# Two transformer layers on one core: whole-tile transposes of the attention output, paired half-zero V copies, first loads from two queues, single-tile GLU at first

## The chip, the core and the metric

The kernel runs on one core of a Trainium2 chip. A core has a matrix engine (PE; its weight loads are shown as PEld), a vector engine (DVE), a scalar engine (ACT), GpSimd (POOL) and a queue engine (SP), which here issues DMAs. Each engine takes its instructions strictly in order; semaphores make one wait for another. The metric is the device time of one execution in microseconds, as the median of several runs.

## What is computed

Two identical layers on a sequence of 2048 rows with 512 features in bf16. Each is attention with 32 heads of 16 features, where a query sees itself and the 255 keys before it, and then a gated MLP of width 1792, each on a layer norm of its input and each added to it:

```python
h = x + A(layernorm(x));  x = h + B(layernorm(h))      # twice, same weights
# A: q, k, v of x @ wqkv; 32 heads of 16
scores = einsum("bhqd,bhkd->bhqk", q, k) * 16 ** -0.5
mask = (i - j >= 0) & (i - j < 256)
o = softmax(where(mask, scores, -1e9)) @ v;  A = o @ wo
# B
B = (sigmoid(x @ w_gate) * (x @ w_up)) @ w_down
```

## The kernel before, in words

The rows are cut into 16 tiles of 128 per layer. All weights and the activations stay in SBUF. Every instruction is laid out by a planner that runs when the program is built (`Plan`, from L169): it keeps a clock of its own, an assumed duration for each instruction and each DMA (`act_ns`, `dve_ns`, `DMA_LATENCY`, `FETCH`, `EXTRA`), and at each step gives an engine the task of the lowest priority number whose inputs are ready on that clock. What it writes down is then the fixed order of each engine. Where the chip is slower than assumed, the engine waits at that place, and all behind it in its order waits too. For a DMA of `ns` and `nbytes` the planner reckons from issue to landing `ns` + EXTRA + bytes/250 + DMA_LATENCY nanoseconds (L230 to L262).

- **Start** (`loads`, L371): tiles 0 to 3 of x come one by one (two DMAs each, even and odd halves of the rows), then wq in three parts, then the rest of x, all issued by SP. GLU weights follow from 18 us of the plan's clock on, one DMA each 1.2 us. Tiles 0 to 3 are normalised (`layer_norm`, L474) and turned on PE (L517); all later ones are turned by a DMA transpose into `xnT` (L529).
- **Projections**: q and k per group of four tiles (L555, L577), v per tile (L609). V is copied into `Vaug`, 18 columns per head: 16 of V and ones, so that the value product also sums the softmax's denominator.
- **Attention**, tile by tile: a *visit* is one round of score products into `Sps` (kinds A at L821, R at L831, S at L841) and one exponential on ACT over 128x2048 scores (L872). A tile has five visits, the last of a layer two. `pick` (L951) does not start a visit before 2.9 or 3.2 us (PACE) have gone by on the plan's clock; other PE work is put between. The kind R gives the edges of the window, which are multiplied with copies of V of which half is zero (`Vlo`, `Vhi`; `half_values`, L1039): per tile two DMAs for each, issued by SP.
- **After the value products** (`values`, L874, half a tile's heads at a time; `after_values`, L905): a copy out of PSUM to `OTs` (L539/L541), a DMA transpose to `Oq` (L916), reciprocal and product on DVE (L922, L923), a DMA transpose to `OnT` (L927). When both halves have come, the output projection (L693) adds to x, and the tile is normalised for the GLU.
- **GLU** (`gate_up_unit`, L627, `down_unit`, L660): units of two tiles, 256 columns wide: eight products into one PSUM bank (L633), tanh on ACT (L644), the product on DVE (L647), and per tile 14 products with w_down (L666). GLU is the filler: it has the lowest rank for PE (`rank`, L1116). So it starts when two tiles have been through attention.
- Where PE has nothing to do within the first 85 us of the plan's clock, four 128-wide products of the identity are put in (`keep_warm`, L1024).

Of the kernel before, what the change touches and what calls it, by code (L numbers as in the profile page):

```python
# [25 lines left out]
VS = 18  # L26
VW = H * VS + 32
UNITS = 8
EDGES = 4
# [71 lines left out]
EXTRA = {"ACT": 40, "DVE": 10, "POOL": 30, "SP": 50}  # L101
# [3 lines left out]
DMA_LATENCY = 1200  # L105
FETCH = (1200, 1300)
# [39 lines left out]
class Task:  # L146


    __slots__ = ("engines", "fn", "prio", "done", "can", "began", "seq", "ends", "port")

    def __init__(self, engines, fn, prio, can, port):
        self.engines, self.fn, self.prio, self.can, self.port = engines, fn, prio, can, port
        self.done, self.began, self.ends = Event(), False, None
# [15 lines left out]
class Plan:  # L169
# [60 lines left out]
    def begin(self, t, e):  # L230
# [9 lines left out]
        if e == "SP":  # L240
# [12 lines left out]
    def count(self, n):  # L253

        if (self.issued + 2 * n) // 256 > self.issued // 256:
            self.fetched = self.now
        self.issued += 2 * n

    def dma(self, ns, nbytes, fn, deps=(), prio=5, after=0):
# [4 lines left out]
        return self.task({"SP": ns}, go, deps, prio, None, after)  # L264
# [30 lines left out]
class Net:  # L295


    def __init__(self, ctx, tc, A_x, wqkv, wo, w_gate, w_up, w_down, out):
# [27 lines left out]
        self.edge = [big.tile([P, 2, H // 2, HP], BF16, name=f"edge{i}") for i in range(EDGES)]  # L326
        self.Vlo = [big.tile([P, VW], BF16, name=f"Vlo{i}") for i in range(2)]
        self.Vhi = [big.tile([P, VW], BF16, name=f"Vhi{i}") for i in range(2)]
# [17 lines left out]
        ring("OTs", 2, [P, 4, P])  # L346
        ring("Oq", 2, [P, 4, P])
        ring("Rt", 2, [P, 4, 4, 1], F32)
        ring("On", 2, [P, 4, 4, 16])
        ring("OnT", 3, [P, 2, P])  # L350
# [20 lines left out]
    def loads(self, A_x, wqkv, wo, w_gate, w_up, w_down):  # L371
# [16 lines left out]
        def load(dst, src, nbytes, after=0, deps=(), prio=2):  # L388
            ns = max(450, 40 + nbytes / 1024 * 0.95)
            return pl.dma(ns, nbytes, lambda: nc.sync.dma_start(out=dst, in_=src), deps, prio, after).done  # L390

        for t in range(NBG):
            self.has_x[t] = load_x(self.xsb[:, t:t + 1, :], slice(t, t + 1), 1, 0)
        for i, k in enumerate("qkv"):
            h = slice(i * D, (i + 1) * D)
            self.has_wq[k] = load(self.wq[:, :, h], wq_src[:, :, h], D * D * 2, prio=0 if k != "v" else 1)
# [5 lines left out]
        gap = 1200  # L402
# [31 lines left out]
    def later_constants(self):  # L434
# [27 lines left out]
        def zeros(e):  # L462
            for i in range(2):
                nc.gpsimd.memset(self.Vlo[i][:], 0.0)
                nc.gpsimd.memset(self.Vhi[i][:], 0.0)
# [3 lines left out]
        self.has_zeros = pl.task({"POOL": 2800}, zeros, prio=7).done  # L469
# [80 lines left out]
    def q_unit(self, L, g, cq):  # L550
# [8 lines left out]
        def evac(u):  # L559
# [3 lines left out]
                self.banks[u.bank][:].rearrange("p (t k z) -> p t z k", z=2, k=HP)), [u.done], 3)  # L563
# [8 lines left out]
    def k_unit(self, L, g, cq):  # L572
# [8 lines left out]
        def evac(u):  # L581
# [12 lines left out]
            a = pl.task({"ACT": act_ns(TGW), "DVE": dve_ns(TGW)}, cp, [u.done], 3, lambda: self.has("kt"))  # L594
            b = pl.task({"DVE": 620}, split, [a.done], 3, port=True)
# [8 lines left out]
    def v_unit(self, L, t):  # L604
# [8 lines left out]
        def evac(u):  # L613
# [3 lines left out]
                e, dst, self.banks[u.bank][:].rearrange("p (i e c) -> p e i c", e=2, c=16)), [u.done, self.has_ones[gi % 3]], 3)  # L617
# [9 lines left out]
    def gate_up_unit(self, L, t0, fc, chunk):  # L627
        nc, pl, key = self.nc, self.pl, ("g", L, t0 // NBG)
        c0 = (t0 % NBG) * P

        def steps(bank):
            pt = self.banks[bank][:].rearrange("p (i w) -> p i w", i=2)
            return [(mm_ns(GW), lambda i=i, w=w, kt=kt: nc.tensor.matmul(  # L633
                pt[:, i, :], lhsT=w[:, kt, fc * P:(fc + 1) * P], rhs=self.xnT[key][0][:, kt, c0:c0 + GW],
                start=kt == 0, stop=kt == KT - 1)) for i, w in enumerate((self.wg, self.wu)) for kt in range(KT)]

        def evac(u):
# [12 lines left out]
            a = pl.task({"ACT": act_ns(GW)}, tanh, [u.done], 2, lambda: self.has("th"))  # L650
            b = pl.task({"DVE": dve_ns(GW)}, mult, [a.done], 1)
            b.done.then(lambda: (self.give(box["th"]), self.h_ready[L, t0, fc].fire()))
            return b.done

        a, b = self.has_gu[fc // 2]
        needs = [self.xn_ready[key, t] for t in range(t0, t0 + GT)] + [a, b, self.h_free[chunk]]
        self.h_free[chunk] = self.h_used[L, t0, fc]
        return Unit(("g", L, t0, fc), steps, needs, True, evac)

    def down_unit(self, L, t, chunks):  # L660
        nc, pl = self.nc, self.pl
        t0 = t - t % GT
        o = (t % GT) * P

        def mm(bank, fc):
            nc.tensor.matmul(self.banks[bank][:], lhsT=self.hT[:, chunks[fc], o:o + P], rhs=self.wd[:, fc, :],  # L666
                             start=fc == 0, stop=fc == FC - 1)
            if t == t0 + GT - 1:
# [20 lines left out]
    def oproj_unit(self, L, t, st):  # L689
        nc, pl = self.nc, self.pl  # L690

        def steps(bank):
            return [(mm_ns(D), lambda c=c: nc.tensor.matmul(  # L693
                self.banks[bank][:], lhsT=st[c // 2][0][:, c % 2, :], rhs=self.wot[:, c, :],
                start=c == 0, stop=c == KT - 1)) for c in range(KT)]

        def evac(u):
            u.done.then(lambda: [self.give(b) for b in st.values()])
# [37 lines left out]
    def visit_exp(self, s):  # L736
# [9 lines left out]
        elif j >= EDGES:  # L746
            i = j - EDGES + 2 if (j - EDGES) % NT < NT - 2 else j - EDGES
            deps += [self.pv_done[divmod(i, NT) + (h,)] for h in range(2)]
# [503 lines left out]
```

## Time and profile before

| | |
|---|---|
| runs | 590.3 us median of 3 (589.15 to 590.78) |
| profiled execution | 593.61 us, of which its trace spans 591.9 us |
| PE busy | 547.8 us, 93% of the span |
| PE weight loads, DVE, ACT, POOL | 364.9, 407.6, 410.2, 64.1 us |
| mean granted PE clock | 0.983 |
| DMA | 38.24 MB in 111752 packets |

A row of a group of instructions gives the line of the code, the engine, the tiles written and read, the count, the busy time in all and the mean length of one, and then the idle time of the engine just before them with what ended it. In the timeline a row begins with its start and its length in us, and an idle stretch stands in brackets. In a table by stages each engine has its busy microseconds within the stage, then come the granted clock, the share of the time in which the DMA engines were busy, and GB/s. Products on PE overlap, so their lengths don't add up; the distance of their starts is read from rows of many in a run.

### The profile page before, as it was taken

To read this page: it belongs to the slowest core of one execution; us is meant where nothing else is said; L and a number is where in the kernel's file an instruction comes from. 1 tells how busy PE (TensorE), PEld (TensorE's weight loads), DVE (VectorE), ACT (ScalarE), POOL (GpSimd) and SP (SyncE) were. 2 spreads that over 40 slices of the span, in tenths; PEclk is the share of its full clock that TensorE was granted. 3 is DMA by queue.
4 is the path that set the end of the run, shared out by engine and by line. 5 is a ranking of instruction groups with operands and counts; after the bars stand their busy time and mean duration, and the time that the engine had idled before them with its cause. 6 is when DMAs were issued, how large, how long until landed. Compare 5 with 4: busy or idle time off the path is not lost.

```text
span 591.9 us, 24275 instructions
## 1 busy us (share of the span) xinstructions
PE 547.8 (93%) x10717; PEld 364.9 (62%) x10808; DVE 407.6 (69%) x931; ACT 410.2 (69%) x480; POOL 64.1 (11%) x149
## 2 busy tenths in 40 slices
PE   6979899998889998998899998999989999999997
PEld 5456577665566666565366664756557665667774
DVE  4838657797766877755877586786667876556642
ACT  2667678887858887876687766867687786765221
POOL 5202101131101111100201002100000000000100
PEclk7979999999989999999999998999999999999999
DMA  6869522232321132113431124212341113213100
GB/s 203 227 164 179 65 55 44 58 65 58 70 53 34 35 57 46 38 43 45 73 64 32 32 56 66 48 26 52 65 85 44 43 35 81 51 44 65 37 19 27
DMA packets 111752, 38.24 MB, mean 65 GB/s; under 512 B 88864, under 2 KB 111648, under 8 KB 111648
## 3 DMA queue, kind: packets, MB, share of 16 engines
q1 hardware_dynamic: 111648, 36.70, 30.1%
q8 instruction: 84, 1.38, 1.0%
q14 instruction: 20, 0.16, 0.1%
HBM read 9.70 MB, written 2.10 MB: 20 GB/s over the span
## 4 chain that ended last, share of the span: by engine, by line
PE 70%; DMA 13%; DVE 7%; ACT 4%; issue 3%; SPq 1%; POOL 1%; DVEq 0%; ACTq 0%
PE bank L633 27%; PE bank L666 11%; PE bank L899 7%; DMA Oq<-OTs 5%; PE bank L555 5%; PE bank L577 5%; PE Sps L821 5%; DMA xnT<-xn 5%; PE bank L693 4%; PE bank L609 3%; DMA OnT<-On 2%; PE bank L1028 2%; PE Sps L831 2%; ACT PTring L872 2%; ACT edge L872 1%
## 5 line engine op out<-in xcount | busy, mean ns | idle before, releaser
L872 ACT ACTIVATE PTring<-Sps 128x2048 bf16<-128x2048 f32 (+1 forms) x122 | 225.9, 1851 | 32.0 <-PE Sps L821 31.4
L633 PE MATMUL bank<-xnT,wg 128*128 128x256 bf16 x896 | 138.5, 274 | 2.3 <-DMA xnT<-xn 1.6
L633 PE MATMUL bank<-xnT,wu 128*128 128x256 bf16 x896 | 139.2, 273 | 0.0
L647 DVE SCALAR_TENSOR_TENSOR hT<-th,bank 128x256 bf16<-128x256 bf16 x224 | 86.9, 416 | 39.2 <-ACT th L644 38.9
L666 PE MATMUL bank<-wd,hT 128*128 128x512 bf16 x395 | 108.4, 380 | 4.8 <-DMA OnT<-On 1.6
L644 ACT ACTIVATE th<-bank 128x256 bf16<-128x256 f32 x224 | 79.7, 389 | 44.2 <-PE bank L633 39.5
L633 PEld LDWEIGHTS <-wg 128*128 128x128 bf16 x896 | 84.1, 98 | 30.1 <-issue 4.6
L633 PEld LDWEIGHTS <-wu 128*128 128x128 bf16 x896 | 86.4, 98 | 14.1 <-issue 1.0
L488 POOL TENSOR_SCALAR st<-st 128x1 f32<-128x1 f32 x64 | 19.6, 306 | 485.6 <-DVE st L484 485.6
L872 ACT ACTIVATE edge<-Sps 128x2048 bf16<-128x2048 f32 (+1 forms) x32 | 56.7, 1772 | 20.8 <-PE Sps L831 20.6
L539 ACT CAST OTs<-bank 128x512 bf16<-128x512 f32 x52 | 38.2, 734 | 46.2 <-PE bank L899 45.2
L666 PEld LDWEIGHTS <-hT 128*128 128x128 bf16 x448 | 42.4, 98 | 37.7 <-DVE hT L647 2.8
L762 DVE TENSOR_TENSOR PTring<-PTring,mask 128x1024 bf16<-128x1024 bf16 x64 | 43.9, 686 | 30.2 <-ACT PTring L872 30.0
L899 PEld LDWEIGHTS <-Vaug 128*32 128x32 bf16 x2880 | 44.9, 97 | 22.3 <-issue 21.0
L899 PE MATMUL bank<-PTring,Vaug 128*32 128x64 bf16 (+1 forms) x2880 | 53.5, 204 | 3.4 <-DVE PTring L762 1.6
L821 PE MATMUL Sps<-qT,kTp 32*128 32x64 bf16 (+3 forms) x1856 | 48.2, 219 | 4.6 <-DMA xnT<-xn 1.9
L483 DVE BATCH_NORM_STATS2 st<-xsb 128x6 f32<-128x512 bf16 x64 | 43.9, 686 | 2.7 <-DMA xsb<-in_A_x_dram 2.2
L762 DVE TENSOR_TENSOR edge<-edge,maske 128x1024 bf16<-128x1024 bf16 x60 | 40.8, 685 | 6.9 <-ACT edge L872 6.9
L899 PE MATMUL bank<-edge,Vlo 128*32 128x64 bf16 x1024 | 45.0, 195 | 0.0
L699 DVE TENSOR_TENSOR xsb<-xsb,bank 128x512 bf16<-128x512 bf16 x32 | 21.9, 685 | 33.2 <-PE bank L693 27.0
L821 PEld LDWEIGHTS <-kTp 32*128 32x128 bf16 x1856 | 24.8, 93 | 29.1 <-issue 25.7
L899 PE MATMUL bank<-edge,Vhi 128*32 128x64 bf16 x896 | 41.3, 194 | 0.0
(61 smaller groups left out, 589.9 us busy)
## 6 DMA issues: line engine op xcount, KB each, us to landing
Vlo<-Vaug SPq DMA_DIRECT2D x64, 36.0 KB, 1.8
out_dram<-xsb SPq DMA_DIRECT2D x32, 64.0 KB, 1.9
Vhi<-Vaug SPq DMA_DIRECT2D x56, 36.0 KB, 2.5
wg<-in_B_w_gate_dram SPq DMA_DIRECT2D x7, 256.0 KB, 3.5
wu<-in_B_w_up_dram SPq DMA_DIRECT2D x7, 256.0 KB, 3.8
wd<-in_B_w_down_dram SPq DMA_DIRECT2D x2, 896.0 KB, 7.2
wq<-in_A_wqkv_dram SPq DMA_DIRECT2D x3, 512.0 KB, 6.2
xsb<-in_A_x_dram SPq DMA_DIRECT2D x6, 256.0 KB, 6.5
```

Of the source, the lines that this page charges most:

```text
L483: nc.vector.bn_stats(out=st[:, 0:6], in_=self.xsb[:, t, :])
L539: self.nc.scalar.copy(out=out, in_=in_)
L555: return [(mm_ns(TGW), lambda kt=kt: nc.tensor.matmul(self.banks[bank][:], lhsT=self.wq[:, kt, cq * P:cq * P + P], rhs=self.xnT[key][0][:, ...
L577: return [(mm_ns(TGW), lambda kt=kt: nc.tensor.matmul(self.banks[bank][:], lhsT=self.wq[:, kt, D + cq * P:D + cq * P + P], rhs=self.xnT[ke ...
L633: return [(mm_ns(GW), lambda i=i, w=w, kt=kt: nc.tensor.matmul(pt[:, i, :], lhsT=w[:, kt, fc * P:(fc + 1) * P], rhs=self.xnT[key][0][:, kt ...
L644: nc.scalar.activation(out=box["th"][0][:], in_=pt[:, 0, :], func=AF.Tanh, scale=0.5)
L647: nc.vector.scalar_tensor_tensor(out=self.hT[:, chunk, :], in0=box["th"][0][:], scalar=1.0, in1=pt[:, 1, :], op0=ALU.add, op1=ALU.mult)
L666: nc.tensor.matmul(self.banks[bank][:], lhsT=self.hT[:, chunks[fc], o:o + P], rhs=self.wd[:, fc, :], start=fc == 0, stop=fc == FC - 1)
L762: done = pl.task({"DVE": dve_bf_ns(1024)}, lambda e: nc.vector.tensor_tensor(out=r, in0=r, in1=m.to_broadcast([P, 16, HP]), op=ALU.mult), ...
L821: nc.tensor.matmul(self.sps[:, m, o:o + n * HP], lhsT=kTp[32 * m:32 * m + 32, i, tt, e, :], rhs=self.qT[32 * m:32 * m + 32, i, q0:q0 + n * ...
L872: nc.scalar.activation(out=out, in_=src, func=AF.Exp, scale=scale)
L899: nc.tensor.matmul(o, lhsT=Va[:, c0:c0 + 32], rhs=p(h), start=k == 0 or t == 0, stop=k == len(parts) - 1 or t == 0, tile_position=(0, 32 * g))
```

## The change

**Turning the attention output.** The two halves of a tile are copied into one `OTs` of 8x128; one DMA transpose turns both (256 KB), one reciprocal and one product follow, and one transpose to `OnT`. `OTs`, `Oq` and `On` have one buffer each instead of two of half the size, `OnT` two instead of three.

**Half-zero V copies.** `Vd` holds two tiles; per pair of tiles two DMAs for the low and two for the high copy, when V of both tiles is there. V takes 17 columns per head instead of 18. The edge tiles are six slots of one tile, with the heads in another order.

**First loads.** ACT issues the three parts of wq, in the order k, q, v; SP issues x in pairs of tiles at the same time. GLU weights come one each 1.6 us.

**GLU.** Tiles 0 and 1 of the first layer are units of one tile: two feature chunks of 128 columns for gate and two for up share a bank, so 16 products of 128 columns instead of 8 of 256. Tanh and product on DVE stay 256 wide.

**The planner's numbers.** Longer DMAs (1500 instead of 1200 ns, 70 instead of 50 per issue), a shorter delay after an instruction fetch but SP held for 900 ns by it, other priorities for copies, up to four GLU units in PSUM instead of three, and projections may be drawn ahead by eight visits instead of six.

```diff
-VS = 18
+VS = 17
-EXTRA = {"ACT": 40, "DVE": 10, "POOL": 30, "SP": 50}
+EXTRA = {"ACT": 40, "DVE": 10, "POOL": 30, "SP": 70}
-DMA_LATENCY = 1200
-FETCH = (1200, 1300)
+DMA_LATENCY = 1500
+FETCH = (1200, 800)
...
             self.fetched = self.now
+            if self.free["SP"] > self.now:
+                self.free["SP"] += 900
...
-        ring("OTs", 2, [P, 4, P])
-        ring("Oq", 2, [P, 4, P])
-        ring("OnT", 3, [P, 2, P])
+        ring("OTs", 1, [P, 8, P])
+        ring("Oq", 1, [P, 8, P])
+        ring("OnT", 2, [P, 4, P])
...
-        for t in range(NBG):
-            self.has_x[t] = load_x(self.xsb[:, t:t + 1, :], slice(t, t + 1), 1, 0)
-        for i, k in enumerate("qkv"):
+        for i, k in enumerate("kqv"):
...
+            self.has_wq[k] = load(self.wq[:, :, h], wq_src[:, :, h], D * D * 2, prio=0, queue="ACT")
+        for t in range(0, NBG, 2):
+            self.has_x[t] = self.has_x[t + 1] = load_x(self.xsb[:, t:t + 2, :], slice(t, t + 2), 2, 0)
...
-        gap = 1200
+        gap = 1600
...
-        b = pl.dma(1190, 131072, turn, [a.done], 3)
+        if half == 0:
+            return
+        b = pl.dma(1800, 262144, turn, [box[0], box[1]], 3)
...
-        d = pl.dma(1190, 65536, turn2, [c.done], 3)
+        d = pl.dma(1190, 131072, turn2, [c.done], 3)
...
+                to, of = dst[e * HP:e * HP + HP, :, e * n:e * n + n], V[z:P:2, o:o + 2, e * n:e * n + n]
+                parts.append(pl.dma(580, HP * n * 4, lambda to=to, of=of: nc.sync.dma_start(out=to, in_=of), deps, 3).done)
...
-                if u.ready() and self.can_go(u) and not (u.on_act and busy_act >= 3):
+                if u.ready() and self.can_go(u) and not (u.on_act and busy_act >= 4):
...
-            return lead / 1000 if lead <= 6 else 6 + lead / 1000
+            return lead / 1000 if lead <= 8 else 6 + lead / 1000
...
+                k = 1 if L * NT + t0 < 2 or L * NT + t0 >= 2 * NT - 0 else 2
+                m = FC * k // 2
...
+                gs += [self.gate_up_unit(L, t0, k, (i,) if k == 2 else (2 * i, 2 * i + 1), chunks[i]) for i in range(m)]
```

What this does to the order of the instructions shows at three places. The first is SP from its first DMA on, before the change (`wg`, `wu`, `wd` are the GLU's weights):

```order
L390 DMA xsb<-in_A_x_dram 64x512 x8
L390 DMA wq<-in_A_wqkv_dram 128x4x512 x3
L390 DMA xsb<-in_A_x_dram 64x4x512 x6
L390 DMA wot<-in_A_wo_dram 128x4x512
L529 DMA_TRANSPOSE xnT_104<-xn_101 128x4x128
L390 DMA wg<-in_B_w_gate_dram 128x4x256
...
L390 DMA wg<-in_B_w_gate_dram 128x4x256
L1050 DMA Vlo_86<-Vaug_77 64x288
L390 DMA wu<-in_B_w_up_dram 128x4x256
L529 DMA_TRANSPOSE xnT_104<-xn_101 128x4x128
```

SP after it:

```order
L394 DMA xsb<-in_A_x_dram 64x2x512 x4
L394 DMA xsb<-in_A_x_dram 64x4x512 x6
L394 DMA wot<-in_A_wo_dram 128x4x512
L1062 DMA Vl_83<-Vaug_77 64x2x272 x2
L1062 DMA Vh_85<-Vaug_77 64x2x272 x2
L394 DMA wg<-in_B_w_gate_dram 128x4x256
L394 DMA wu<-in_B_w_up_dram 128x4x256
L536 DMA_TRANSPOSE xnT_101<-xn_98 128x4x128
```

The wq loads have left SP, and the V copies of tiles 0 and 1 stand ahead of every GLU weight; before, the first of them stood behind five. The second place is ACT at its first copies, before:

```order
L539 COPY xnT_103<-bank_64 128x4x128
L539 COPY xnT_103<-bank_65 128x4x128
L539 COPY xnT_103<-bank_66 128x4x128
L539 COPY xnT_103<-bank_67 128x4x128
L539 CAST kt_106<-bank_64 128x512
L539 CAST qT<-bank_65 128x512
```

and after:

```order
L394 DMA wq<-in_A_wqkv_dram 128x4x512 x3
L546 ACT_TABLE_LOAD
L546 COPY xnT_100<-bank_64 128x4x128
L546 COPY xnT_100<-bank_65 128x4x128
L546 CAST Vaug_77<-bank_66 128x32x16
L546 COPY xnT_100<-bank_67 128x4x128
L546 CAST Vaug_77<-bank_64 128x32x16
L546 CAST kt_103<-bank_67 128x512
```

V of tiles 0 and 1 now comes ahead of the first k and q. The third is ACT at its first tanh (`th`), before; the exponential of `edge` in these rows belongs to tile 4, whose number is the fifth edge written:

```order
L539 CAST Vaug_79<-bank_65 128x32x16
L872 ACTIVATE PTring<-Sps 128x16x128 x3
L644 ACTIVATE th_108<-bank_67 128x256
L644 ACTIVATE th_109<-bank_64 128x256
L644 ACTIVATE th_110<-bank_65 128x256
L872 ACTIVATE edge_82<-Sps 128x4x8x64
```

and after, where the `edge` is that of tile 3:

```order
L883 ACTIVATE PTring<-Sps 128x8x2x128 x2
L546 CAST Vaug_79<-bank_64 128x32x16
L883 ACTIVATE PTring<-Sps 128x8x2x128
L653 ACTIVATE th_105<-bank_65 128x256
L883 ACTIVATE edge<-Sps 128x4x2x256
L653 ACTIVATE th_106<-bank_66 128x256
```

Before, 20 exponentials stand ahead of the first tanh, 19 visits ahead of the first gate product; after, 15 and 15.

More of the change, by code (lines that the diff above doesn't have):

```diff
@@ L256, in count, with dma @@
             self.fetched = self.now
+            if self.free["SP"] > self.now:
+                self.free["SP"] += 900
+                self.at(self.free["SP"])
         self.issued += 2 * n
-    def dma(self, ns, nbytes, fn, deps=(), prio=5, after=0):
+    def dma(self, ns, nbytes, fn, deps=(), prio=5, after=0, queue="SP"):
         def go(e):
@@ L262, in go @@
             self.dma_free = max(self.dma_free, self.now + ns) + nbytes / 250.0
-        return self.task({"SP": ns}, go, deps, prio, None, after)
+        t = self.task({queue: ns}, go, deps, prio, None, after)
+        t.transfer = True
+        return t
     def run(self, pe):
@@ L745, in visit_exp @@
             deps += [self.ring_free(L, t, h) for h in range(2)]
[L746 to L749 removed]
+        elif j >= 2:
+            deps += [self.pv_done[divmod(j - 2, NT) + (h,)] for h in range(2)]
+        x = pl.task({"ACT": EXP_NS}, lambda e: self.exp(L, t, kind, i), [d for d in deps if d is not None], 1)
         U = UNIT[j]
@@ L906, in after_values @@
         nc, pl = self.nc, self.pl
-        box = {}
+        box = self.outs.setdefault((L, t), {})
         def move(e):
-            box["OTs"] = self.take("OTs")
-            self.copy(e, box["OTs"][0][:].rearrange("p c (k z) -> p c z k", z=2),
+            if "OTs" not in box:
+                box["OTs"] = self.take("OTs")
+            self.copy(e, box["OTs"][0][:, 4 * half:4 * half + 4, :].rearrange("p c (k z) -> p c z k", z=2),
                       self.banks[bank][:].rearrange("p (c z k) -> p c z k", z=2, k=HP))
```

169 lines of the change are left out of this document (87 added, 82 removed).

## Prediction

> **What bounds the kernel now.** I read the stages first, then PE's waits, then the timeline where the stages differ. The stages (columns: length; busy time of PE, weight loads, DVE, ACT, POOL; clock; DMA share; GB/s):
>
> ```profile
> 0.00:83.00 83.00, 70.00 (x1261) 46.53 (x1271) 54.16 (x126) 51.30 (x47) 17.83 (x49) 0.92 0.69 155
> 83.00:550.00 467.00, 440.36 (x9191) 291.79 (x9266) 336.36 (x767) 348.95 (x407) 44.70 (x96) 0.99 0.26 52
> 550.00:592.00 42.00, 37.45 (x270) 26.58 (x272) 17.10 (x38) 9.96 (x26) 1.58 (x4) 1.00 0.10 27
> ```
>
> From 83 us on PE is busy for 440.36 of 467 us, ACT for 75%: PE is the bound there and in the tail. The first stage looks busy too, but a table of the identity products alone shows what that is:
>
> ```profile
> 16.00:83.00 67.00, 19.49 (x284) 17.18 (x284) 0.00 (x0) 0.00 (x0) 0.95 0.69 142
> 83.00:592.00 509.00, 1.01 (x12) 0.76 (x12) 0.00 (x0) 0.00 (x0) 0.99 0.25 50
> ```
>
> 284 of them fill PE until there is GLU work, and almost none are needed after. The timeline gives the first projection, a run of 40 fillers, the first gate product and a round of scores; the chain gives gate and down products back to back:
>
> ```profile
> 12.19 0.61 PE L577 MATMUL bank<-xnT,wq 128*128 128x512 bf16 x1
> 50.58 2.41 PE L1028 MATMUL bank<-ident 128*128 128x128 bf16 x40
> 82.65 0.49 PE L633 MATMUL bank<-xnT,wg 128*128 128x256 bf16 x3
> 83.07 0.40 PE L821 MATMUL Sps<-qT,kTp 32*128 32x64 bf16 x16
> 572.95 1.75 PE bank L633 x16
> 581.24 3.02 PE bank L666 x14
> ```
>
> So a 128-wide product takes about 58 ns (2.41 less the last one's length of 0.2, over 39, is 57), a 256-wide one 109 ns (1.75/16), and a 512-wide one 216 (3.02/14). The sum of PE's useful work is fixed; the end comes earlier by what PE stops losing, before 82.65 us in waits and fillers, after it in waits. These are its waits that end with a DMA or with what a late DMA held up (who waited for whom; total, times, longest):
>
> ```profile
> PE bank L693 <- DMA OnT<-On: 6.9, 4, 3.4
> PE bank L555 <- DMA xnT<-xn: 3.0, 2, 2.0
> PE bank L1028 <- ACT Vaug L539: 2.1, 1, 2.1
> PE Sps L821 <- DMA xnT<-xn: 1.9, 1, 1.9
> PE bank L666 <- DMA OnT<-On: 1.6, 1, 1.6
> PE bank L633 <- DMA xnT<-xn: 1.6, 4, 0.7
> PE Sps L821 <- ACT PTring L872: 1.4, 1, 1.4
> ```
>
> **Part by part, as time on PE.** *First loads.* SP spends 5.06 us issuing x and only then issues wq:
>
> ```profile
> 0.79 5.06 SPq L390 DMA_DIRECT2D xsb<-in_A_x_dram  x8
> 5.89 1.69 SPq L390 DMA_DIRECT2D wq<-in_A_wqkv_dram  x3
> 8.35 2.51 DVE L505 TENSOR_SCALAR xn<-xsb,st 128x512 bf16<-128x512 bf16 x4
> 9.43 1.56 ACT L539 COPY xnT<-bank 128x512 bf16<-128x512 bf16 x3 [7.36 <-PE bank L517]
> 5.00:6.00 1.00, 1.00 (x21) 0.97 (x18) 0.95 (x6) 0.00 (x0) 0.61 (x1) 1.00 0.27 75
> 9.00:10.00 1.00, 1.00 (x12) 1.00 (x11) 0.86 (x3) 0.57 (x2) 1.00 (x4) 0.50 1.10 390
> ```
>
> The wq issues cost ACT 1.7 us inside its 7.36 us of idleness; without that cover, the 1.7. But DVE, 0.95 busy in 5:6, sets the last xn (10.9 us) as much as the loads do, and five V products now stand between the last turned tile and the first k. I take 1 us of gain. Ends: 3 us gained if PE no longer falls to half clock here (0.50 in 9:10; twelve 512-wide products at 216 instead of twice that are 2.6), 2 lost if ten V products at half clock (4.3 us) are only half covered. DMA engines were 0.27 busy in 5:6, so the queue that issues was the narrow place. The Trainium skill (DMA: Bandwidth & Descriptors, "Issuing engines are not separate DMA queues") says a second issuing engine saves only the sequencer's time, since all transfers share the same DMA engines; by it this part saves at most the 5.06 us of issues that stand before wq's now. The 1.10 share in 9:10 agrees that the transfers then crowd each other, and DVE's part leaves 1 of it.
>
> *V copies ahead of the GLU weights.* Now SP places the first copy of V among the 256 KB loads:
>
> ```profile
> 25.60 0.54 SPq L1050 DMA_DIRECT2D Vlo<-Vaug  x1
> 29.98 1.07 ACT L539 CAST Vaug<-bank 128x512 bf16<-128x512 f32 x2 [4.25 <-DMA Vlo<-Vaug]
> 32.89 0.61 PE L821 MATMUL Sps<-qT,kTp 32*128 32x128 bf16 x24 [1.44 <-ACT PTring L872]
> 33.43 2.74 PE L1028 MATMUL bank<-ident 128*128 128x128 bf16 x24
> 35.97 0.63 PE L555 MATMUL bank<-xnT,wq 128*128 128x512 bf16 x1
> 36.82 1.49 PE L555 MATMUL bank<-xnT,wq 128*128 128x512 bf16 x3 [0.22 <-issue]
> 34.00:36.00 2.00, 2.00 (x22) 2.00 (x20) 0.54 (x1) 1.43 (x1) 0.00 (x0) 0.50 0.81 230
> ```
>
> It lands 4.3 us after its issue; ACT's next V copy waits for it, idle for 4.25 us, and behind that copy stand the exponentials on which PE's scores wait. Then PE runs at half clock: 24 fillers in 2.74 instead of 1.5 us, four q products in 0.63 + 1.49 instead of 0.86, 2.5 us lost. After the change the copies of tiles 0 and 1 (SP order above) are issued when V of both is there, ahead of the weights. Gain 4.2 + 2.5 = 6.7. Lower end: nothing, if ACT's copies still wait.
>
> The half clock came after PE had been idle for 2.1 us (its wait for `Vaug` above) and 1.44 us within five; I take it that without those waits it does not come.
>
> *GLU of single tiles.* The order has 228 fillers between the first score and the first gate product where 284 stood: 56 x 58 ns = 3.3 us gained. For two tiles, 224 products of 128 columns (13.1 us) replace 112 of 256 (12.2): 0.9 lost. Lower end of the pair: 0.9 lost, if xnT of tile 0 is late; upper 3.3 gained, if the narrow products fall into idle time.
>
> *Whole-tile turning.* The issues and landings of today:
>
> ```profile
> L916 SPq DMA_TRANSPOSE Oq<-OTs x64: 1189/1218/2030, 39.7 to 544.3; - x64
> L927 SPq DMA_TRANSPOSE OnT<-On x64: 1167/1181/3106, 46.4 to 548.8; - x64
> L1050 SPq DMA_DIRECT2D Vlo<-Vaug x64: 464/547/1617, 25.6 to 528.1; - x64
> Oq<-OTs SPq DMA_TRANSPOSE x64, 2.5
> OnT<-On SPq DMA_TRANSPOSE x64, 2.4
> L922 DVE RECIPROCAL Rt<-Oq 128x16 f32<-128x16 bf16 x64 | 15.9, 248 | 23.2 <-DMA Oq<-OTs 23.2
> L923 DVE TENSOR_TENSOR On<-Oq,Rt 128x256 bf16<-128x256 bf16 x64 | 27.2, 425 | 2.7 <-DMA OnT<-On 0.5
> ```
>
> SP issues 64 x 1.22 + 64 x 1.18 + 120 x 0.55 = 220 us of these; after, 32 turns of unknown length (1.2 if size is free as from 64 to 128 KB, 2.4 if it doubles) + 32 x 1.2 + 60 x 0.55, so 110 to 148. An emptier SP lets fewer transposes queue behind others. Against it: a turn now waits for the second half and lands later. The planner's reserve tells when that hurts: 1190 + 50 + 524 + 1200 = 2.96 us today for a landing of 2.5; 1800 + 70 + 1049 + 1500 = 4.42 after. The 256 KB landing is not in the trace: 2.4 against 2.5 us for double the size suggests 2.6 to 3, proportion would give 5.0. I take about 3, so the reserve covers it, and OnT, at 128 KB like Oq today, lands in 2.5 against 3.3. PE's DMA waits in the list (6.9 + 1.6 + 3.0 + 1.9 + 1.6 = 15.0) shrink, but xnT's remain and some OnT waits come from one transpose held behind another, so I take 2.5 gained of 15.0; ends 15 gained, 18.6 lost (next part). DVE saves about 43.1 - 32 x 0.95 = 13 us in all, hidden behind PE. ACT's first copy of a tile now waits until the previous turn has landed (one `OTs`), with exponentials behind it and PE's scores waiting for those; halves come (544.3 - 39.7)/63 = 8.0 us apart, more than the landing, so it costs nothing; without that cover, up to a landing of 2.5 to 5 us less those 8.
>
> By the Trainium skill (DMA: Bandwidth & Descriptors, "Latency and other measured facts", DMA transposes at 261 GB/s), the added 128 KB would be an estimated 0.5 us, a landing of 3.0. By that figure the sum is the same.
>
> *At nothing*: the memsets of zeros (POOL is 11% busy), the edges' order of heads (same 128x2048 exponential), priorities, eight visits, the fourth unit in PSUM. All act on who fills PE; the cover is the GLU backlog. Where it fails, they cost or give a microsecond or two.
>
> Sum: -1 - 6.7 - 3.3 + 0.9 - 2.5 = -12.6. The profiled execution's 593.6 (span 591.9 and 1.7 around it) becomes 581.0; the runs' median lies 3.3 lower, so 577.7.
>
> **Rivals.** (1) *The turn's landing is late*: price 32 projections x (landing - 4.42). At 5.0 that is 18.6 us if PE has nothing else in its fixed order: -1 - 6.7 - 3.3 + 0.9 + 18.6 = +8.5, so 598.8, slower; it decides from (landing - 4.42) x 32 > 10.1, a landing of 4.74. Against it speak 2.4 and 2.5 us for 64 and 128 KB. Chance 0.07.
> (2) *The odd stride of V*: with 17 columns every second head's V starts two bytes off a four-byte boundary.
>
> ```profile
> 184.68 0.87 PE bank L899 x80
> ```
>
> If every second value product took double, a block of 80 would cost 0.4 more, 64 blocks 26 us: 603. No run shows it. Chance 0.04.
> (3) *The copies of V still hold ACT up* behind 2 MB of x and wo, which SP now has ahead of them: without the 6.7, 584.4. For it: the DMA share of 1.10 in 9:10. Against: those loads are issued within the first microseconds. Chance 0.22.
> (4) *Given back*: GLU begins earlier, but one tile's worth (9 us of PE) runs out within a tile's five visits, PE starves later, and the time stays within 0.3% of 590.3. For it: ACT is 75% busy and paced, so attention can't be hurried. Against: only 12 fillers are ordered after the first gate product. Chance 0.10.
> (5) *Forecast*: 0.57.
>
> **The numbers.** 577.7. A measurement of this kernel tells about 0.3% from no change, 1.8 us. Forecast and rival 3 are faster, and I allow a little of 4 to be as well: 0.80 faster, 0.09 the same, 0.11 slower. Range: upwards through rival 3 and into 4, to 590; downwards DMA waits and start at their good ends would give -3 - 6.7 - 3.3 + 0.9 - 15 = -27, not all at once; I take two thirds of the step from -12.6 to -27, so 568.
>
> **What would show it.** The first gate product near 63 us: 82.65 less 8.5 us of work that now comes later (by the order 24 products of 216 ns, two value blocks of 0.87, four rounds of scores of 0.40) and 11 us of loss. No wait of ACT for a V copy near 25 us. A 256 KB landing between 2.6 and 4.4. PE's waits for OnT and xnT under 15.0. The block of 80 still at 0.87. Wrong would be: the first gate product after 72 us, OnT waits that grow, or an unchanged end in spite of an early first gate product.

## The result, and the profile after

The changed kernel takes 563.8 us (median of 4 runs, 562.4 to 566.1) where the kernel before took 590.5 in the runs beside it: a ratio of 0.954, 95% interval 0.948 to 0.960. It is faster, as forecast, but by 26.7 us and not by 12.6, so the time lies below the range. The profiled execution of 562.5 us has a span of 560.8; it is set against the 593.6 and 591.9 of before. Ratios leave disturbed executions out, so that the ratio and the median of one run below (before_stirred_2) say different things.

The page, busy time and granted clock, and the stages (columns as in the prediction):

```profile
PE 545.8 (97%) x10880; PEld 361.6 (64%) x10880; DVE 398.2 (71%) x864; ACT 410.3 (73%) x483; POOL 68.1 (12%) x157
PEclk9999999999999999999999999999999999999999
```

```profile
0.00:83.00 83.00, 76.46 (x1540) 52.70 (x1541) 61.27 (x135) 57.61 (x58) 21.71 (x59) 1.00 0.63 158
83.00:520.00 437.00, 432.79 (x9078) 283.15 (x9076) 321.29 (x696) 343.07 (x401) 45.61 (x96) 1.00 0.30 55
```

In the long middle stage PE is now busy 432.79 of 437 us (99%), against 440.36 of 467 (94%). The middle is where most of the unforecast gain lies. In this execution the clock no longer drops anywhere. The identity products alone, and the timeline at the first gate product:

```profile
16.00:62.00 46.00, 14.94 (x228) 13.09 (x228) 0.00 (x0) 0.00 (x0) 1.00 0.75 177
62.00:83.00 21.00, 0.83 (x12) 0.75 (x12) 0.00 (x0) 0.00 (x0) 1.00 0.19 36
```

```profile
61.56 0.61 PE L641 MATMUL bank<-xnT,wg 128*128 128x128 bf16 x8
```

The first gate product starts at 61.56 (forecast: near 63), after 228 fillers. PE's waits, the whole list (who waited for whom; total, times, longest):

```profile
PE bank L524 <- DVE xn L512: 4.5, 4, 2.2
PE bank L641 <- DMA xnT<-xn: 1.7, 2, 1.1
PE bank L1039 <- POOL ident L428: 1.4, 1, 1.4
PE Sps L841 <- ACT PTring L883: 1.2, 4, 0.5
PE Sps L831 <- ACT PTring L883: 0.8, 1, 0.8
PE bank L674 <- ACT OTs L546: 0.3, 1, 0.3
```

There is no wait for `OnT` any more, and 1.7 us for `xnT`: of the 15.0 us of before, 13.3 are gone. What is also gone are PE's waits for DVE after the first gate product, 7.4 us in the list of before, of which these are the largest, and two stretches at half clock:

```profile
PE bank L555 <- DVE PTring L762: 2.4, 1, 2.4
PE bank L899 <- DVE PTring L762: 1.6, 2, 1.3
PE bank L899 <- DVE hT L647: 1.1, 1, 1.1
PE bank L633 <- DVE hT L647: 0.7, 2, 0.5
```

```profile
165.30:168.70 3.40, 3.40 (x120) 2.45 (x118) 2.44 (x6) 2.15 (x2) 0.79 (x2) 0.50 0.05 12
359.90:363.30 3.40, 3.40 (x40) 1.33 (x39) 0.84 (x2) 2.29 (x2) 0.00 (x0) 0.50 0.49 97
```

DVE was late in part because it stood in its own order before transposes that had not landed. One case of the kernel before, in its timeline:

```profile
442.31 0.25 DVE L922 RECIPROCAL Rt<-Oq 128x16 f32<-128x16 bf16 x1 [2.67 <-DMA Oq<-OTs]
442.94 0.69 DVE L762 TENSOR_TENSOR PTring<-PTring,mask 128x1024 bf16<-128x1024 bf16 x1
443.67 0.21 PE L899 MATMUL bank<-PTring,Vaug 128*32 128x64 bf16 x4 [1.34 <-DVE PTring L762]
```

DVE stands for 2.67 us before a turned tile, the mask behind it comes late, and PE waits 1.34 us for the mask. Of the 7.4 us, 3.7 follow such a stand by less than 6 us. In the longest wait (2.4) the mask that is named had been done for 0.5 us, so something else ended it; before the remaining 1.2 DVE had waited for exponentials. DVE's whole wait for the turned tile was 23.2 us (the reciprocal's row in the prediction, "23.2 <-DMA Oq<-OTs"). It is now 2.5, by the list of DVE's waits:

```profile
DVE Rt L934 <- DMA Oq<-OTs: 2.5, 5, 0.7
```

The tile `Oq` has the issues (ns min/median/max, first and last start), and the list of DMA issues the landings (median us, last column):

```profile
L928 SPq DMA_TRANSPOSE Oq<-OTs x32: 1232/1264/2205, 38.3 to 511.0; - x32
```

```profile
Oq<-OTs SPq DMA_TRANSPOSE x32, 3.2
OnT<-On SPq DMA_TRANSPOSE x32, 2.5
```

A turn of 256 KB takes SP 1.26 us to issue, where 128 KB took 1.22, and lands in 3.2.

**Where the 31 us went.** PE's time is split at the first gate product: useful work (the products of the order, each kind at one price in every run: 216, 109 and 56 ns for 512, 256 and 128 columns, 10.9 for a value product, 0.35 us for a round of scores), fillers at 57 ns, and the rest, which is what PE lost. The differences between runs don't hang on the prices.

| us | before | after | difference |
|---|---|---|---|
| rest before the first gate product | 21.5 | 11.1 | -10.4 |
| fillers, whole run | 20.5 | 18.2 | -2.3 |
| rest after it | 40.0 | 21.3 | -18.7 |
| useful work, whole run | 509.8 | 510.1 | +0.3 |

The waits after the first gate product account for the 18.7: waits for a DMA went from 12.1 to 1.7 us, waits for DVE from 7.4 to none, the two slow stretches cost 3.4, and waits for ACT grew from none to 2.3. That makes -18.9, without PE's "issue" gaps.

### The profile page after: what moved, and what is told of

The parts are those of the page before. It is cut to its first block, busy times and chain, and to the rows that moved or that the text cites. A ratio compares the mean times of both kernels' runs of the same rounds, so it can differ in the third digit from the quotient of the medians.

```text
span 560.8 us, 24161 instructions
## 1 busy us (share of the span) xinstructions
PE 545.8 (97%) x10880; PEld 361.6 (64%) x10880; DVE 398.2 (71%) x864; ACT 410.3 (73%) x483; POOL 68.1 (12%) x157
## 4 chain that ended last, share of the span: by engine, by line
PE 83%; DVE 5%; DMA 4%; ACT 4%; issue 2%; POOL 1%; SPq 0%; ACTq 0%; DVEq 0%; POOLq 0%
PE bank L641 32%; PE bank L674 17%; PE bank L910 8%; PE Sps L831 6%; PE bank L701 5%; PE bank L562 5%; PE bank L616 4%; PE bank L584 4%; ACT PTring L883 3%; DMA xnT<-xn 2%; PE Sps L841 2%; DVE st L490 1%; DVE PTring L769 1%; DMA xsb<-in_A_x_dram 1%; DMA Oq<-OTs 1%
## 5 line engine op out<-in xcount | busy, mean ns | idle before, releaser
L641 PE MATMUL bank<-xnT,wg 128*128 128x256 bf16 (+1 forms) x952 | 139.4, 267 | 1.8 <-DMA xnT<-xn 1.7
L641 PE MATMUL bank<-xnT,wu 128*128 128x256 bf16 (+1 forms) x952 | 140.0, 267 | 0.0
L674 PE MATMUL bank<-wd,hT 128*128 128x512 bf16 x448 | 112.3, 380 | 0.3 <-ACT OTs L546 0.3
L641 PEld LDWEIGHTS <-wg 128*128 128x128 bf16 x952 | 85.9, 98 | 27.2 <-issue 5.0
L641 PEld LDWEIGHTS <-wu 128*128 128x128 bf16 x952 | 87.9, 98 | 14.0 <-issue 1.4
L883 ACT ACTIVATE edge<-Sps 128x2048 bf16<-128x2048 f32 (+1 forms) x32 | 56.8, 1775 | 12.7 <-PE Sps L841 12.5
L546 ACT CAST OTs<-bank 128x512 bf16<-128x512 f32 x49 | 36.0, 735 | 35.8 <-PE bank L910 32.7
L910 PEld LDWEIGHTS <-Vaug 128*32 128x32 bf16 x2880 | 44.4, 97 | 17.2 <-issue 15.5
L910 PE MATMUL bank<-edge,Vl 128*32 128x64 bf16 x1024 | 44.6, 193 | 0.0
L831 PEld LDWEIGHTS <-kTp 32*128 32x128 bf16 x1856 | 24.7, 92 | 27.3 <-issue 23.9
L496 POOL TENSOR_TENSOR st<-st,nhalf 128x1 f32<-128x1 f32 x64 | 41.0, 641 | 5.3
L910 PE MATMUL bank<-edge,Vh 128*32 128x64 bf16 x896 | 41.1, 193 | 0.0
```

The lines of the kernel that those rows point to most:

```text
L496: nc.gpsimd.tensor_tensor(out=st[:, 8:9], in0=st[:, 9:10], in1=self.nhalf[:], op=ALU.pow)
L546: self.nc.scalar.copy(out=out, in_=in_)
L641: return [(mm_ns(w), lambda i=i, j=j, fc=fc, wt=wt, kt=kt: nc.tensor.matmul(pt[:, i, j, :], lhsT=wt[:, kt, fc * P:(fc + 1) * P], rhs=self. ...
L674: nc.tensor.matmul(self.banks[bank][:], lhsT=self.hT[:, c, o:o + P], rhs=self.wd[:, fc, :], start=fc == 0, stop=fc == FC - 1)
L831: nc.tensor.matmul(self.sps[:, m, o:o + n * HP], lhsT=kTp[32 * m:32 * m + 32, i, tt, e, :], rhs=self.qT[32 * m:32 * m + 32, i, q0:q0 + n * ...
L883: nc.scalar.activation(out=out, in_=src, func=AF.Exp, scale=scale)
```

## The experiments

Four theories are named in the expectations. **R**: the planner's larger reserve for a DMA (1500 for 1200 ns) places the consumers of transposes later, so that PE and DVE, which run a fixed order, stop standing before late ones. **Q**, the rival: the emptier queue of SP did it, with 32 pairs of transposes and 60 V copies for 64 and 120. **S**: the new first loads crowd each other, so that the old ones would bring the first score forward and the end with it. **O**: one order was luckier than another. The column "Oq" of the table is DVE's wait for the turned tile; "PE, DMA" is PE's wait for `OnT` and `xnT` in the whole run; "rest" is PE's loss after the first gate product. What a variant of the kernel before gains or loses is taken to the kernel before beside it, whose median was 590.2 to 591.5 us; a variant of the changed kernel is set against the 563.8 of the result, and by the ratios of the table, which go by the runs beside, those differences come out within 2 us of the ones named.

| run | us (range) | ratio, 95% | first gate | rest | PE, DMA | Oq |
|---|---|---|---|---|---|---|
| before | 590.5 | 1 | 82.6 | 40.0 | 15.0 | 23.2 |
| before_stirred | 603.3 (595.9-603.7) | 1.021, 1.014-1.029 | 78.2 | 46.6 | 13.8 | 35.7 |
| before_stirred_2 | 595.1 (586.4-597.1) | 1.001, 0.996-1.006 | 83.3 | 39.0 | 12.0 | 27.3 |
| hold_only | 583.8 (581.5-589.5) | 0.990, 0.982-0.998 | 83.6 | 40.0 | 12.5 | 20.7 |
| latency_only | 578.4 (576.0-580.6) | 0.981, 0.973-0.989 | 83.2 | 25.6 | 6.9 | 15.9 |
| latency_stirred | 579.5 (578.1-580.5) | 0.979, 0.973-0.985 | 83.8 | 29.5 | 9.9 | 13.3 |
| before_1800 | 578.5 (577.9-581.4) | 0.979, 0.971-0.987 | 82.2 | 26.4 | 5.7 | 10.2 |
| plan_only | 576.7 (573.9-579.5) | 0.976, 0.969-0.983 | 83.7 | 28.0 | 4.4 | 10.1 |
| after_old_plan | 574.3 (571.3-576.2) | 0.972, 0.965-0.978 | 69.7 | 26.8 | 5.1 | 6.6 |
| after_1200 | 571.2 (569.8-572.4) | 0.965, 0.959-0.971 | 65.7 | 26.2 | 5.2 | 5.2 |
| single_v | 573.1 (571.5-576.9) | 0.973, 0.966-0.979 | 67.3 | 27.4 | 6.3 | 7.3 |
| old_priorities | 572.4 (569.6-575.8) | 0.970, 0.962-0.977 | 66.0 | 29.7 | 5.6 | 8.1 |
| half_turns | 570.3 (568.5-571.7) | 0.967, 0.961-0.972 | 72.1 | 24.5 | 4.9 | 7.4 |
| two_tile_glu | 569.7 (568.6-570.3) | 0.964, 0.958-0.970 | 76.9 | 22.7 | 4.5 | 1.5 |
| after_stirred | 565.7 (563.2-566.8) | 0.959, 0.953-0.964 | 61.7 | 21.9 | 2.2 | 1.7 |
| old_loads | 564.6 (563.9-566.0) | 0.957, 0.951-0.964 | 65.8 | 22.0 | 3.1 | 2.4 |
| after | 563.8 (562.4-566.1) | 0.954, 0.948-0.960 | 61.6 | 21.3 | 1.7 | 2.5 |
| reserve_1800 | 563.0 (562.2-564.1) | 0.953, 0.948-0.959 | 65.5 | 19.6 | 1.1 | 1.5 |

### The planner's reserves alone, and without them

plan_only is the kernel before with the three numbers and the hold; after_old_plan is the changed kernel with all of it back.

```
-EXTRA = {..., "SP": 50}       +EXTRA = {..., "SP": 70}
-DMA_LATENCY = 1200            +DMA_LATENCY = 1500
-FETCH = (1200, 1300)          +FETCH = (1200, 800)
+            if self.free["SP"] > self.now:
+                self.free["SP"] += 900
+                self.at(self.free["SP"])
```

> The kernel before with the planner's new numbers for DMAs alone (reserve 1500 instead of 1200 ns, 70 instead of 50 per issue on SP, the fetch delay, SP held for 900 ns by a fetch); every operation is as before. Theory R (longer reserves put PE's consumers of a transpose later in the fixed order, so nothing waits): the 18 us that the stage after the first gate product gained come along, 590.5 - 18 = 572, and PE's waits for OnT and xnT fall from 15.0 to under 5 us. Rival Q (the emptier SP queue does it, 189 instead of 285 rows): 590 within 4 us, waits for OnT and xnT still over 10 us.

> The changed kernel with the planner's old numbers for DMAs (1200, 50, fetch 1300, SP not held). Theory R: most of the 18 us goes back, 578 to 584, with PE waits for OnT and xnT over 10 us. Rival Q: 564 within 4 us, waits under 5 us.

The reserves alone gave 14.8 us and did not bring the first gate product forward (83.7). Without them the changed kernel lost 10.5 us and still kept 17.2. Both R and Q hold a part, and neither foretold the second run: its 574.3 us and 5.1 us of waits lie between R's 578 to 584 with over 10 and Q's 564 within 4. The first came 4.7 us above R's 572, with the waits (4.4) as R said.

### A touch that means nothing

```
-EXTRA = {..., "DVE": 10, ...}     +EXTRA = {..., "DVE": 12, ...}
```

> Control: the kernel before with a number of the planner that means nothing here changed (12 instead of 10 ns added per DVE instruction), so that the same operations stand in a slightly different order. Both theories: 590 within 4 us; how far it is off tells how much a reordering alone is worth.

> Control: the changed kernel with 12 instead of 10 ns added per DVE instruction in the plan. If longer reserves and an emptier queue make the order robust: 564 within 3 us, where the same touch moved the kernel before by 12. If orders differ by luck as much as before: off by up to 12.

The kernel before went up by 11.8 us (603.3 against 591.5 beside it), three times the 4 expected, the changed one by 1.8. The trace shows only a part of this: it is of the shortest execution, 595.9 us at a granted clock of 0.994, where the other four took 602.8 to 603.7 at 0.979 to 0.983. In it DVE's wait for the turned tile grew from 23.2 to 35.7 us, while PE's waits for transposes stayed near those of before, 13.8 for 15.0 (PE's, then DVE's):

```profile
PE bank L633 <- DMA xnT<-xn: 5.7, 4, 3.0
PE bank L693 <- DMA OnT<-On: 4.0, 4, 1.5
PE bank L555 <- DMA xnT<-xn: 2.9, 1, 2.9
PE bank L899 <- DVE PTring L762: 2.9, 5, 1.1
DVE Rt L922 <- DMA Oq<-OTs: 35.7, 23, 3.6
```

So a gain of some 12 us in one variant of the kernel before proved nothing yet: theory O was open until the last four runs.

### The parts of the plan apart

latency_only is the kernel before with the second of the four edits, hold_only with the other three.

> The kernel before with the DMA reserve 1500 instead of 1200 ns alone. If the reserve per DMA carries what the new numbers gave (590 to 577): 575 to 581, PE's waits for OnT and xnT under 6 us. If the hold of SP at a fetch carries it: 586 to 596.

> The kernel before with the other new numbers for DMAs, without the reserve: 70 per issue, the shorter fetch delay, SP held 900 ns by a fetch. If the reserve carries the gain: 584 to 596, within what a stir does. If the hold does: 575 to 581.

The reserve for a DMA alone gave 11.8 us on an unchanged set of instructions; the rest after the first gate product fell from 40.0 to 25.6, and PE's waits for transposes to 6.9, a little over the 6 expected. The others gave 6.3, just more than expected if the reserve carries the gain, but little beside what a mere touch can do. They left the rest at 40.0; ahead of the first gate product it is 12.9 for 21.5, with 80 more fillers (4.6 us). The waits of latency_only (PE's, then DVE's):

```profile
PE bank L555 <- DMA xnT<-xn: 3.8, 3, 1.4
PE bank L693 <- DMA OnT<-On: 1.7, 4, 0.8
DVE Rt L922 <- DMA Oq<-OTs: 15.9, 16, 2.8
```

### Reserve or luck

Four more kernels: the reserve alone with the touch as well (DVE 12), the reserve at 1800 in the kernel before, the reserve back at 1200 in the changed kernel, and a second touch of the kernel before (DVE 9).

```
 latency_stirred   DMA_LATENCY = 1500, EXTRA "DVE": 12   (kernel before)
 before_1800       DMA_LATENCY = 1800                    (kernel before)
 after_1200        DMA_LATENCY = 1200                    (changed kernel)
 before_stirred_2  EXTRA "DVE": 9                        (kernel before)
```

> The kernel before with the reserve for a DMA at 1500 and the planner's DVE overhead at 12 instead of 10, so another order with the same reserve. Theory R (the reserve itself): again 574 to 584 us, with under 30 us of time that is neither useful work nor fillers after the first gate product, and under 9 us of PE waits on OnT and xnT, as with the reserve alone. Theory O (the gain of the reserve alone was luck of one order): anywhere from 585 to 603, as the kernel before went to 603 by the same touch.

> The kernel before with the reserve for a DMA at 1800 instead of 1200. Theory R: 572 to 582, with under 6 us of PE waits on OnT and xnT, since the longer reserve covers more of the landings' tail. Theory O: anywhere from 580 to 603, without a trend in the reserve.

> The changed kernel with the reserve for a DMA alone back at 1200. Theory R: 569 to 576, and 3 to 6 us of PE waits on OnT and xnT where the changed kernel has 1.7. Rival Q (SP's emptier queue did it, the reserve matters little once the queue is empty): 562 to 567.

> The kernel before with the planner's DVE overhead at 9 instead of 10, which means nothing by itself. Theory R: 585 to 605, with over 9 us of PE waits on OnT and xnT, since the reserve is still 1200. Theory O: anywhere from 575 to 605; a time under 582 would show that a meaningless touch can give what the reserve gave.

With the kernel before's instructions, the four orders with 1200 have medians of 584 to 603 us, and the four with 1500 or 1800 of 577 to 579; every execution of the second group (573.9 to 581.4) is shorter than every one of the first (581.5 to 603.7), though at the edge by no more than 0.1 us. Four pairs differ in the reserve alone: before and latency_only (11.8 us), before_stirred and latency_stirred (23.8), hold_only and plan_only (7.1), after_1200 and the changed kernel (7.4). The clock is not the cause either: the executions at a granted clock of 0.994 to 0.998 take 581.5 to 595.9 us with 1200 and 573.9 to 579.5 with more. So theory O is refuted as the cause of the whole gain. The order still counts: the touch that cost 11.8 us at 1200 costs 1.0 at 1500, and the worth of the reserve runs from 7 to 24 us with the order. The waits of latency_stirred came out at 9.9, a little over the 9 that R allowed. A reserve of 1800 gives no more than 1500 does. In the changed kernel the reserve alone is worth 7.4 us, as R said and Q did not; its waits come back (PE's, then DVE's):

```profile
PE bank L701 <- DMA OnT<-On: 3.0, 4, 1.2
PE bank L562 <- DMA xnT<-xn: 1.3, 2, 0.7
PE bank L641 <- DMA xnT<-xn: 0.9, 1, 0.9
DVE Rt L934 <- DMA Oq<-OTs: 4.2, 5, 1.7
```

### Single parts undone in the changed kernel

half_turns turns each half tile by itself again; single_v copies V one tile at a time, 120 copies for 60.

```
 half_turns (with after_values and oproj_unit of the kernel before)
-        ring("OTs", 1, [P, 8, P])
-        ring("Oq", 1, [P, 8, P])
-        ring("OnT", 2, [P, 4, P])
+        ring("OTs", 2, [P, 4, P])
+        ring("Oq", 2, [P, 4, P])
+        ring("OnT", 3, [P, 2, P])
 single_v (per tile, not per pair of tiles)
+                parts.append(pl.dma(450, HP * n * 2, lambda o=o, i=i: nc.sync.dma_start(out=o, in_=i), deps, 3).done)
```

> The changed kernel with the attention output turned by halves again (64 transposes to Oq and 64 to OnT), all else as changed, the long reserves too. If the emptier SP queue carries a part of the gain through the turns: 569 to 576, with losses after the first gate product between the 21.3 us of the changed kernel and the 28.0 of the kernel before with new reserves. If the reserves and the early GLU are all: 564 within 4 us.

> The changed kernel with V copied per tile again (120 DMAs instead of 60). If the pairs matter through SP's load: 567 to 572. If they matter only in that the first copies come early, the first gate product moves by up to 4 us and the time with it. If the turns and the reserves are all: 564 within 4 us.

Half turns cost 6.4 us, single copies 9.3, a little more than the 567 to 572 expected. These are Q's part: the same planner, more transfers. Half turns also give DVE twice the reciprocals and products (it is busy for 403.1 us instead of 398.2), so that run does not separate SP's queue from DVE's work. The landings of the half turns have a longer tail than the whole ones, as far as they are in the trace (36 of 64 and 20 of 32; rows of the tile `Oq`, first of half_turns, then of the changed kernel):

```profile
DMA to landing us min/median/max: 2.4/2.8/7.6
```

```profile
DMA to landing us min/median/max: 3.0/3.2/4.9
```

With single copies DVE stands before V's copies too:

```profile
DVE Rt L934 <- DMA Oq<-OTs: 6.2, 6, 2.0
DVE Vaug L548 <- DMA Vh<-Vaug: 3.4, 1, 3.4
DVE Vaug L548 <- DMA Vl<-Vaug: 2.9, 2, 1.9
```

two_tile_glu runs the first two tiles of the GLU together again; old_loads has the first loads of the kernel before.

```
 two_tile_glu
-                k = 1 if L * NT + t0 < 2 or L * NT + t0 >= 2 * NT - 0 else 2
+                k = 2
 old_loads (in place of wq from ACT's queue and x by two tiles)
+        for t in range(NBG):
+            self.has_x[t] = load_x(self.xsb[:, t:t + 1, :], slice(t, t + 1), 1, 0)
+        for i, k in enumerate("qkv"):
+            h = slice(i * D, (i + 1) * D)
+            self.has_wq[k] = load(self.wq[:, :, h], wq_src[:, :, h], D * D * 2, prio=0 if k != "v" else 1)
```

> The changed kernel with GLU in units of two tiles from the start. If the early first gate product is worth what fillers it saves: the first gate product falls from about 61 to about 75 us and the time rises by 4 to 9 us, to 568 to 573. If the early start is given back later: 564 within 2 us. Theories R and Q say nothing of it.

> The changed kernel with the old first loads (x tile by tile, then wq, all by SP). Theory S (the loads from two queues crowd each other: x lands at 7.2 instead of 3.7 us, the first score comes at 19.4 instead of 16.3): the first score comes at 15 to 17 us and the time falls by 2 to 4 us, to 560 to 562. Rival (the start doesn't count, since fillers wait for the attention's pace anyway): 564 within 1.5 us.

Single tiles are worth 5.8 us: without them 56 more fillers (3.2 us) and 3.8 us more of other loss stand before the first gate product, at 76.9. The loads of before bring the first score forward by 4.7 us and the end by nothing that stands out of the runs' spread (564.6 for 563.8). What they give comes back a little later, as ACT's wait for a V copy (the timeline's first score and SP's first V copy, then ACT's wait):

```profile
14.68 0.41 PE L831 MATMUL Sps<-qT,kTp 32*128 32x128 bf16 x24
24.01 1.35 SPq L1062 DMA_DIRECT2D Vl<-Vaug  x1
```

```profile
ACT Vaug L546 <- DMA Vl<-Vaug: 3.8, 1, 3.8
```

Theory S falls with it: its earlier first score came, its shorter time did not.

old_priorities puts the ranks of the changed kernel back; reserve_1800 raises its reserve further.

```
 old_priorities: exponential and tanh rank 2, q/k/v copies 3, lead <= 6, busy_act >= 3
 reserve_1800:   -DMA_LATENCY = 1500    +DMA_LATENCY = 1800
```

> The changed kernel with the old priorities for tanh, exponential and copies, three GLU units in PSUM and projections six visits ahead. If these rules carry a part: 567 to 573, with waits of PE for tanh, for h or for a bank. If they don't: 564 within 3 us.

> The changed kernel with a DMA reserve of 1800 ns. Theory R, still short of what landings need: 558 to 562. If the waits that can go are gone (PE's list is down to 1.7 us for xnT and nothing for OnT): 562 to 567, since PE's consumers come later and nothing waits less.

The ranks, the eight visits and the fourth unit cost 8.6 us when undone. PE then waits for exponentials (4.5 us in these two rows, 2.0 in the changed kernel), and for transposes 5.6 us instead of 1.7:

```profile
PE Sps L841 <- ACT PTring L883: 2.9, 5, 2.0
PE Sps L831 <- ACT PTring L883: 1.6, 3, 0.9
```

A reserve of 1800 leaves 1.1 us of PE's waits for transposes instead of 1.7 and moves the time by 0.9 us, within the runs' spread: there is no more to be had here, and none of these kernels clearly beats the changed one. Every run of a kernel with one part undone, the loads aside, is longer than every run of the changed kernel and of its touched copy (562.4 to 566.8 against 568.5 and up), so each of these parts is needed. They don't add: 7.4 + 6.4 + 9.3 + 5.8 + 8.6 is 37.5, more than the 26.7 of the whole, so they overlap.

## Why the forecast was right in sign and short in size

*V copies ahead of the GLU weights, and fillers: right.* The first gate product came at 61.6 for 63. Fillers fell by 2.3 us and the rest ahead of it by 10.4, 12.7 together, where the prediction's steps had 10 (6.7 + 3.3) and 1 for the loads. ACT has no wait for a V copy, and the clock is 1.00 where it fell to 0.50.

*First loads: wrong in sign for the start, nothing in time.* x lands later, in loads of twice the size and with wq beside them; no run separates the two. The start of the changed kernel:

```profile
0.78 1.59 ACTq L394 DMA_DIRECT2D wq<-in_A_wqkv_dram  x3
7.22 0.69 DVE L490 BATCH_NORM_STATS2 st<-xsb 128x6 f32<-128x512 bf16 x1 [2.94 <-DMA xsb<-in_A_x_dram]
10.02 0.64 POOL L463 MEMSET Vaug<- 128x128 bf16 x1
10.11 2.16 DVE L512 TENSOR_SCALAR xn<-xsb,st 128x512 bf16<-128x512 bf16 x1 [0.47 <-POOL st L496]
17.17 1.30 SPq L1062 DMA_DIRECT2D Vl<-Vaug  x2
19.42 0.41 PE L831 MATMUL Sps<-qT,kTp 32*128 32x128 bf16 x24
```

DVE's first statistics begin at 7.22 and the first score at 19.42, where old_loads has 14.68. So the first score comes 4.7 us later by the new loads, where the prediction had 1 us gained and at most 2 lost. The time differs by 0.8 us, within the spread: old_loads has the wait for V back (3.8 us), so the two terms hang together. With the new loads the first V copies are issued at 17.17, ahead of the GLU weights, and with the old ones at 24.01, among them. The Trainium skill (DMA: Bandwidth & Descriptors, "Issuing engines are not separate DMA queues") says that a second issuing engine brings no second set of DMA engines. This case agrees: wq is issued at 0.78 instead of 5.89, and x lands later.

*Narrow products and single tiles: right for what was counted.* The products cost 0.9 or less (useful work grew by 0.3 in all, by the prices above). Single tiles bring 5.8, where 3.3 - 0.9 stood: the fillers, 3.2, came as costed, and the 3.8 us of other loss ahead of the first gate product had not been counted.

*Whole-tile turning: the step that failed.* It is "some OnT waits come from one transpose held behind another, so I take 2.5 gained of 15.0". 13.3 of the 15.0 went, and with them 7.4 us of waits for DVE and 3.4 us of half clock that the prediction did not count at all. The cause that it names is there. Of the 38.0 us for which PE and DVE stood before these transposes in the kernel before, 20.3 ended with a landing that took longer than the plan reckons from the issue (2.91 us for `Oq` and `xnT`, 2.65 for `OnT`); in the other 17.7 the landing was within that, and what was late was the issue, or work before it. PE's longest wait is of this kind:

```profile
158.36 0.42 DVE L923 TENSOR_TENSOR On<-Oq,Rt 128x256 bf16<-128x256 bf16 x1
158.50 3.63 SPq L529 DMA_TRANSPOSE xnT<-xn  x2
162.23 1.19 SPq L927 DMA_TRANSPOSE OnT<-On  x1
164.64 0.61 PE L693 MATMUL bank<-wot,OnT 128*128 128x512 bf16 x2 [3.36 <-DMA OnT<-On]
```

`On` is done at 158.78, SP is at two transposes of `xnT` until 162.13, and `OnT` lands 2.36 us after its issue, which is not slow.

Two things were wrong in the step. First, its size: an edit that reckons 0.3 us more for every DMA moves every consumer of `xnT`, `Oq` and `OnT` back in its order, and so takes in late issues as well as slow landings. The prediction read the edit from 1200 to 1500 only as the arithmetic of rival 1 (4.42 against a landing). Alone it gives 11.8 us, and the change without the planner's new numbers gains 17.2 (after_old_plan), which is nearer to the 12.6 that were added up. Second, DVE's 23.2 us of waiting for `Oq` stood in a quoted row, and the prediction took DVE's savings as "hidden behind PE". But DVE works in a fixed order too. While it stands before a late tile, the masks and GLU products behind it are late, and PE waits for those, as at 443.67 above. In the four orders with the reserve of 1200 and the old instructions, DVE's wait for `Oq` is 20.7 to 35.7 us and PE's rest 39.0 to 46.6; in the four with more, 10.1 to 15.9 and 25.6 to 29.5.

*At nothing: wrong.* The ranks, the visits and the fourth unit were costed at nothing or "a microsecond or two". Undone, they cost 8.6.

*The range.* The prediction's good ends add up to 27 us, and 26.7 were measured. That they meet is partly luck: the waits for transposes gave 13.3 of the 15 in that sum, but the 3 us of the first loads did not come, and DVE's waits, the half clock after the first gate product and the ranks were not in it. The lower edge of 568 came from taking two thirds of the step to those ends.

*Rivals.* (1) A late landing decided from 4.74 us; it is 3.2. The reckoning behind it, and the formula that was given for the planner, count a term too much: the code takes the longer of `ns` + EXTRA and `ns` + bytes/250 and then adds DMA_LATENCY, so 2.91 us before and 4.35 after, not 2.96 and 4.42, and the rival would have decided from 4.67. The Trainium skill's figure for transposes (DMA: Bandwidth & Descriptors, "Latency and other measured facts") gave the estimate of 3.0, and this trace agrees within 0.2. (2) The odd stride of V costs nothing; the blocks of 80 in the chain take 0.91 to 0.97, where they took 0.87 to 1.04; two of them:

```profile
154.53 0.94 PE bank L910 x80
213.39 0.96 PE bank L910 x80
```

(3) ACT's wait for V is gone. (4) Nothing was given back: after 61.6 us there are 12 fillers (0.83 us).

What stays open: how the 18.7 us divide between reserve and emptier queue. The reserve gives 11.8 in the old kernel and 7.4 in the new one, so the two overlap, and no run gives a single share. The order of the edges was not undone alone. Why some transposes land in 5 to 9 us when the median is 2.5 was not tried either, nor why the clock is lower in some executions of one and the same kernel.

## What to carry to other kernels

Where engines run a fixed order, the latency that the planner reckons for a transfer is a lever of its own: set it to cover late issues and slow landings and not the median landing, and look at the engines behind PE that stand before transfers, since their waits come out as PE's waits elsewhere. An edit to a planner's constant moves every consumer, so it deserves a term of the sum with both ends, above all when the waits that it can remove are in the list (here 15 us). Before a difference of one variant is believed, touch the kernel in a way that means nothing: here that alone moved the kernel before by 11.8 us.

## What the runs showed of the hardware that was not expected

- The issue of a transpose hardly depends on its size: 1.18 us (`OnT`, 64 KB), 1.22 (128 KB) and 1.26 (256 KB), with landings of 2.4, 2.5 and 3.2.
- One DVE operation over 128x512 took 2.16 us at 10.11 beside memsets of POOL that run from 10.02 on, where the same operation just before, at 9.23, took 0.41.
- With the first loads split over two queues, the one that is wanted first came later: 128 KB of x landed in 5.0 us with wq beside it, 64 KB in 2.1 without (medians of the changed kernel and of old_loads).
